# Two decoder layers over a long key and value cache, one core: queries by halves of w_q, finer loads between the layers, keys turned two quarters at a time

## The chip, the core and the metric

The kernel runs on one core of a Trainium2 chip. The metric is device time in microseconds (us) for one execution; smaller is better. The kernel before takes 649.24 us in the median of three runs (648.29 to 649.81). The engines are called TensorE (PE in the profile), VectorE (DVE), ScalarE (ACT), GpSimd (POOL) and SyncE (SP). SyncE issues all DMAs; sixteen DMA engines carry them out, each a sixteenth of every large load.

## The reference

Four sequences of one token each (x is 4 x 512) go through attention, a feed-forward block, and both once more with the same weights and the same cache:

```python
x = x + attention(layernorm(x), k_cache, v_cache, wq, wo)
x = x + ffn(layernorm(x), w_gate, w_up, w_down)
x = x + attention(layernorm(x), k_cache, v_cache, wq, wo)
x = x + ffn(layernorm(x), w_gate, w_up, w_down)

# attention: 32 query heads, 8 key/value heads, 8192 cached positions, head size 128
q = x @ wq                          # 4 x (32 x 128)
p = softmax(q k^T * 128 ** -0.5)    # a group of 4 query heads shares one key head
return (p @ v) @ wo

# ffn: inner size 1792
return (silu(x @ w_gate) * (x @ w_up)) @ w_down
```

All tensors are bfloat16. The keys and values of all sequences are 67 MB each and are needed in both layers; the little that on-chip memory can keep from one layer to the next is kept, the rest is read twice. Nearly all of the 273 MB that the kernel reads is keys and values.

## The kernel before

**Tiles and slots.** The work of a layer is 16 units; a unit u is one sequence and two key heads (`pair_gb`). Its keys K(L, u) and its values V(L, u) are one tile each of 128 partitions by 32 KB (4096 KB). On chip, `kvf` has four slots of that size and a fifth, number `QS`, which holds w_q until the second layer's queries are made and is a fifth slot of the ring from then on. Each slot is divided into eight blocks (`NB = 8`, "quarters" in the change's words), named `s<slot>.<block>`; a block is 512 KB. A small remainder behind the slots holds part of w_up. The feed-forward weights of layer 0 and 1 go into the slots `W_SLOT = (1, 3)`.

**Order of the loads.** `cmds` (L346 to L364) is a list, written out once, of all loads in order: tile, slot, first and last block. `pump` (L405) issues from its head as long as the blocks that the next load needs are free, and stops at the first that is not; so all loads keep this order on SyncE's queue. `freed(s, a, b)` marks blocks free and pumps; it is called in the program where the last reader of those blocks has been emitted, and the load then waits on semaphores for that reader. At the change of layers the list goes: the weights of layer 0's feed-forward, the second keys' tile of layer 1 into slot 1 (as 3, 1 and 4 blocks), the third into slot `QS` (as 4 and 2 blocks), the fourth into slot 0 (as 4 and 4), the third unit's predecessor's values into slot 1 (as 4 and 4), and then whole tiles in turn.

**What is kept between the layers.** The order of units in layer 1 begins with the last ones of layer 0 (`order`, L322). The keys of the last unit stay in slot 0, turned already, and become layer 1's first tile; two values' tiles stay too. Of one more keys' tile, K(0, NP - 3), the last two blocks are moved into PSUM by `hold(q, False)`, and brought back into slot `QS` by `hold(q, True)` after the queries of layer 1 are made. Bringing back overwrites w_q's place, so it waits for what was last recorded on the names "wq0" and "wq1" (`WQ`):

```python
if back:                                                              # L450
    T._wait("dve", T._need((), WQ))
    T.op("dve", lambda e: e.transpose(w, banks), reads=there, writes=here)   # L452
```

`_need` (L31) collects, for each name, its last writer and the readers since. A name's last writer is whatever operation or load listed it last in `writes`; `load` (L424) lists both names of `WQ` with the first load that goes into slot `QS`.

**A unit's keys.** `keys` (L598) takes a tile's eight blocks in turn. VectorE turns a block in place (`turn`, L488: 32 x 32 transposes of 4-byte words, 128 x 1024); TensorE then makes the scores of that block with four matmuls (`scores`, L512) into one PSUM bank. After the eighth block VectorE takes the maximum (L518), TensorE turns it (L523), VectorE reduces it (L526), TensorE spreads it (L554, later L549), VectorE forms the bias (L557), ScalarE the exponentials (L559), and VectorE turns those (L576). `values` then multiplies them with the values' tile (L643), VectorE gathers the parts (L689, L693). The scores of a block run behind its turning by a lag (`LAG`, and `AHEAD` for the second tile of layer 1, which lets all its eight blocks be turned first); `line` holds the small steps above and spaces them by estimated times. Every engine takes its instructions strictly in the emitted order.

**Queries.** `qproj` (L833) makes the queries of all heads: for each of 32 heads four matmuls over the four 128-row parts of w_q (L839), two of which lie in each half of the slot. In the middle stands `deviation` (L826), the layer norm's scale. In layer 0 it waits for both loads of w_q.

**Feed-forward.** `ffn` (L861) does gate, up (L876) and down (L907, in three groups of `WDS`) and frees blocks 0 to 2 after gate, block 3 after up, and blocks 4 to 7 after all of down. In layer 1 the down matmuls are those of L897.

Of the kernel before, what the change touches and what calls it, by code (L numbers as in the profile page):

```python
# [9 lines left out]
FP32 = mybir.dt.float32  # L10
# [93 lines left out]
def bass_interleave_layers__gqa_block_cached__swiglu_ffn__decode_kernel(  # L104
# [20 lines left out]
    KT = D // P  # L125
# [19 lines left out]
    with ExitStack() as es:  # L145
# [50 lines left out]
        def room(s, a, b):  # L196
            return [f"s{s}.{q}" for q in range(a // BW, (b - 1) // BW + 1)]
# [137 lines left out]

        ends = lambda it, s: [(it, s, 0, QH), (it, s, QH, NB - 1), (it, s, NB - 1, NB)]
        half = lambda it, s: [(it, s, q, q + NB // 2) for q in range(0, NB, NB // 2)]

        def placed(seq, ring, parts):
            out = []  # L340
            for i, it in enumerate(seq):
                s = ring[i % len(ring)]
                out += parts[i](it, s) if i in parts else [(it, s, 0, NB)]
            return out
# [10 lines left out]

        us = order[1]
        s = W_SLOT[0]
        cmds += [(K(1, us[1]), s, 0, 3), (K(1, us[1]), s, 3, 4), (K(1, us[1]), s, 4, NB)]
        cmds += [(K(1, us[2]), QS, 0, NB // 2), (K(1, us[2]), QS, NB // 2, NB - 2)]
        seq = loads(1, 3)  # L360
        ring = (0, 1, 3, QS, 2)
        cmds += placed(seq, ring, {0: half, 1: half, len(seq) - 1: ends})
        assert W_SLOT[1] == ring[len(seq) % len(ring)]
        cmds += [(("W", 1), W_SLOT[1], 0, NB), (("W+", 1), W_SLOT[1], NB, NB + 1)]  # L364

# [58 lines left out]
        def load(it, a, b, sm):  # L424
            kind, L, u = it
            s = slot_of[it]
            gp, bt = pair_gb(u)
            src = (A_k_cache if kind == "K" else A_v_cache)[bt, 2 * gp:2 * gp + 2, :, :].rearrange(
                "h (p t) d -> (h p) (t d)", t=TT)
            over = WQ if s == QS and not q_gone else []  # L430
            q_gone.update(over)
            T.dma("sp", kv[:, s, a * BW:b * BW], src[:, a * BW:b * BW], sm,
                  writes=[f"s{s}.{q}" for q in range(a, b)] + over)
# [46 lines left out]
                line.pop(0)[2]()  # L480


        def turn(L, u, q):


            s = slot_of[K(L, u)]
            w = kv[:, s, q * BW:(q + 1) * BW].bitcast(FP32)
            T.op("dve", lambda e: e.transpose(w, w), reads=[f"s{s}.{q}"], writes=[f"s{s}.{q}"])  # L488
            turned.add((L, u, q))

        placed_q = set()

# [105 lines left out]
        def keys(L, u, before, lag):  # L598
            def block(q):
                if q == 0:  # L600
                    place_q(L, u)
                scores(L, u, q)
                finished(K(L, u), q, q + 1)
                if q == NB - 1:
                    step = lambda gap, fn: [gap, u, lambda: fn(u)]
                    line.extend([step(0.0, max_p), step(1.2, max_t)])
                    after = [step(0.9, exps), step(1.3, lambda u: turn_p(L, u))]
                    if u == order[L][-1]:
                        after = [after[0], step(0.3, lambda u: turn_p(L, u)), [2.5, None, lambda: total(u)]]
                    (line if before is None else behind.setdefault(before, [])).extend(after)  # L610

            drain(lag)
            for q in range(NB):
                if (L, u, q) not in turned:
                    turn(L, u, q)
                blocks.append((0.9, lambda q=q: block(q)))
                drain(lag)

# [213 lines left out]

        def qproj(L, u):  # L833
            at, name = place("ln", 0, Hq * B)
            for h in range(Hq):
                if h == Hq // 2:
                    deviation(lsc_sb, "lsc")
                for kt in range(KT):
                    T.op("pe", lambda e: e.matmul(at[:, h * B:(h + 1) * B],  # L839
                                                  lhsT=wq_sb[:, kt, h * Dh:(h + 1) * Dh],  # L840
                                                  rhs=xn[:, kt * B:(kt + 1) * B],
                                                  start=(kt == 0), stop=(kt == KT - 1)),
                         reads=[f"wq{kt // 2}", "xn"], writes=[name], sig=(kt == KT - 1))
# [14 lines left out]
            place_q(L, u, "dve", ob, [oname])  # L858
            T.op("dve", lambda e: e.tensor_copy(qr, ob), reads=[oname], writes=["qr", "made"])

        def ffn(L):  # L861
# [3 lines left out]
            uT = bank(ub)[:, 0:FO * B]  # L865
            fb = lambda ap: ap.rearrange("p (f b) -> p f b", b=B)
            rb = rstd[:].unsqueeze(1).to_broadcast([P, FO, B])
            rooms = {"wg": room(s, 0, O_WU), "wu": room(s, O_WU, O_WD), "wd": room(s, O_WD, O_WD + FO * D)}
            names = {"wg": ["wg"], "wu": ["wu0", "wu1", "wu2"]}
            for at, wname, bk in ((wg_at, "wg", gb), (wu_at, "wu", ub)):  # L870
                for fo in range(FO):
# [19 lines left out]
            if L == 1:  # L891
                x_rows(1)
                for i, (a, b, _) in enumerate(WDS[1]):
                    for fo in range(a, b):
                        for j in range(NA):
                            o = s * SL + O_WD + fo * D + j * P
                            T.op("pe", lambda e: e.matmul(quarter(j), lhsT=hT[:, fo * B:(fo + 1) * B],  # L897
                                                          rhs=kvf[:, o:o + P], start=False, stop=(fo == FO - 1)),
                                 reads=["hT", f"wd{i}"] + rooms["wd"], writes=[f"part{j}"],
                                 sig=(fo == b - 1))  # L900
                freed(s, 4, NB)
                return
            for j, (a, b, _) in enumerate(WDS[0]):
                k = OBK[0] if j else SBK[1]
                for nt in range(KT):
                    for fo in range(a, b):
                        T.op("pe", lambda e: e.matmul(bank(k)[:, nt * B:(nt + 1) * B],  # L907
                                                      lhsT=wd_at(s, fo, nt),
                                                      rhs=hT[:, fo * B:(fo + 1) * B],
                                                      start=(j < 2 and nt == 0 and fo == a),  # L910
                                                      stop=(j in (0, NW - 1) and nt == KT - 1 and fo == b - 1)),
                             reads=["hT", f"wd{j}"] + rooms["wd"], writes=[f"pb{k}"], sig=(fo == b - 1))
                if not j:
                    add_to_x(bank(k)[:, 0:XB], f"pb{k}")
            freed(s, 4, NB)
            add_to_x(bank(k)[:, 0:XB], f"pb{k}")


# [10 lines left out]
        for L in range(2):  # L929
            us = order[L]  # L930
            turn_of.update((u, i % 2) for i, u in enumerate(us))
            totals.clear()
            mixed.clear()
            center()
            qproj(L, us[0])
            if L:
                for q in (NB - 2, NB - 1):
                    hold(q, True)
                freed(QS, 0, NB - 2)
            todo = [("K", 0)]  # L940
# [51 lines left out]
```

## Time and profile before

| what | value |
|---|---|
| median of three runs | 649.24 us (648.29 to 649.81) |
| the profiled execution | 648.29 us |
| its span, first to last instruction | 646.5 us |
| read from HBM | 272.9 MB, 422 GB/s over the span |
| DMA queue of SyncE | busy 99.0% of 16 engines' span |
| PE, DVE busy | 425.6 us (66%), 430.1 us (67%) |
| mean granted TensorE clock | 0.876 |
| L488, a block turned | 246 times, 1219 ns each |
| L512, a score matmul | 1024 times, 426 ns each |

The profile divides the span into 40 slices of 16.2 us; layer 0's attention ends at about 339 us, its feed-forward runs from there to 351 us, the queries of layer 1 from 352.6 to 357 us. In a group of instructions the first number is busy time, then the mean of one in ns; the idle time stands after the bar, with what ended most of it. In the chain of waits each line is a start, a length, and the engine, tile and line. For DMAs the number behind the size is the median time from the issue on SyncE to the landing on the last of the DMA engines, which includes the time that a load waits behind others.

### The profile page before, as it was taken

To read this page: it belongs to the slowest core of one execution; us is meant where nothing else is said; L and a number is where in the kernel's file an instruction comes from. 1 tells how busy PE (TensorE), PEld (TensorE's weight loads), DVE (VectorE), ACT (ScalarE), POOL (GpSimd) and SP (SyncE) were. 2 spreads that over 40 slices of the span, in tenths; PEclk is the share of its full clock that TensorE was granted. 3 is DMA by queue.
4 is the path that set the end of the run, shared out by engine and by line. 5 is a ranking of instruction groups with operands and counts; after the bars stand their busy time and mean duration, and the time that the engine had idled before them with its cause. 6 is when DMAs were issued, how large, how long until landed. Compare 5 with 4: busy or idle time off the path is not lost.

```text
span 646.5 us, 7503 instructions
## 1 busy us (share of the span) xinstructions
PE 425.6 (66%) x3128; PEld 173.1 (27%) x3128; DVE 430.1 (67%) x706; ACT 41.2 (6%) x117; POOL 11.1 (2%) x43
## 2 busy tenths in 40 slices
PE   2574466556766755767757987777665576657878
PEld 2221122212322212222226332222222222222225
DVE  1585467566776666777852878888766677766953
ACT  1000000000000000001010010000000000000110
POOL 0000000000000000000000000000000000000000
PEclk9996896789787999878985799999878997789977
DMA  9999999999999999999999999999999999999996
GB/s 363 445 423 416 442 429 430 426 435 433 426 430 435 430 425 436 435 422 436 434 407 409 396 435 434 434 429 423 442 427 426 433 438 424 431 440 423 430 417 268
DMA packets 14129, 273.37 MB, mean 423 GB/s; under 512 B 1416, under 2 KB 1424, under 8 KB 5264
## 3 DMA queue, kind: packets, MB, share of 16 engines
q1 hardware_dynamic: 14096, 272.91, 99.0%
q8 instruction: 24, 0.39, 0.2%
q14 instruction: 9, 0.07, 0.0%
HBM read 272.90 MB, written 0.00 MB: 422 GB/s over the span
## 4 chain that ended last, share of the span: by engine, by line
DMA 61%; DVE 26%; PE 9%; issue 3%; SPq 0%; ACT 0%; DVEq 0%
DMA kvf<-in_A_k_cache_dram 49%; DVE kvf L488 20%; DMA kvf<-in_A_v_cache_dram 10%; PE ps L512 3%; DVE pT L576 3%; PE ps L643 2%; DMA kvf<-in_B_w_down_dram 2%; DVE pb L693 2%; PE ps L839 1%; DVE pb L689 0%; PE ps L876 0%; DVE scr L703 0%; DVE kvf L452 0%; PE ps L759 0%; SPq L93 0%
## 5 line engine op out<-in xcount | busy, mean ns | idle before, releaser
L512 PE MATMUL ps<-kvf,zq 128*128 128x512 bf16 x1024 | 298.0, 426 | 181.1 <-DVE kvf L488 174.3
L488 DVE STREAM_TRANSPOSE kvf<-kvf 128x1024 f32<-128x1024 f32 x246 | 289.8, 1219 | 108.6 <-DMA kvf<-in_A_k_cache_dram 107.7
L512 PEld LDWEIGHTS ps<-kvf,zq 128*128 128x128 bf16 x1024 | 90.6, 105 | 350.9 <-DVE kvf L488 257.8
L643 PE MATMUL ps<-kvf,pT 128*32 128x512 bf16 x960 | 66.7, 400 | 1.4 <-DVE pT L576 0.8
L559 ACT ACTIVATE pb<-ps,tiny 128x512 bf16<-128x512 f32 x32 | 22.0, 688 | 531.8 <-DVE tiny L557 495.2
L576 DVE STREAM_TRANSPOSE pT<-pb 64x512 bf16<-64x512 bf16 x60 | 41.2, 687 | 3.1 <-ACT pb L559 2.0
L518 DVE TENSOR_REDUCE tiny<-ps 128x1 f32<-128x512 f32 x32 | 22.0, 687 | 31.6 <-PE ps L512 31.6
L693 DVE SCALAR_TENSOR_TENSOR pb<-ps,tiny,pb 128x128 f32<-128x128 f32 x104 | 36.5, 351 | 5.1 <-PE ps L643 1.3
L643 PEld LDWEIGHTS ps<-kvf,pT 128*32 128x32 bf16 x960 | 20.8, 98 | 31.9 <-issue 15.7
L698 PEld LDWEIGHTS ps<-sel,pb 128*128 128x128 f32 x64 | 15.4, 258 | 21.3 <-DVE pb L693 14.0
L502 POOL TENSOR_TENSOR zq<-scr,tiny 128x64 bf16<-128x64 bf16 x30 | 9.0, 300 | 564.8 <-PE ps L512 564.8
L526 DVE TENSOR_REDUCE mrm<-ps 1x8 f32<-1x128 f32 x32 | 8.8, 275 | 14.2 <-PE ps L523 14.2
L698 PE MATMUL ps<-sel,pb 128*128 128x8 f32 x64 | 12.7, 272 | 8.1 <-DVE pb L693 8.1
L549 PEld LDWEIGHTS ps<-mrm,tiny 128*128 128x128 f32 x60 | 12.0, 205 | 8.6 <-DVE scr L703 3.2
L759 PE MATMUL ps<-wo_sb,scr 128*4 128x512 bf16 x48 | 11.0, 379 | 1.5 <-DVE scr L728 1.5
L689 DVE TENSOR_SCALAR pb<-ps,tiny 128x128 f32<-128x128 f32 x32 | 10.1, 315 | 2.6 <-PE ps L643 2.6
L549 PE MATMUL ps<-mrm,tiny 128*128 128x16 f32 x60 | 9.3, 231 | 3.1 <-ACT mrm L561 3.1
L839 PE MATMUL ps<-xn,kvf 128*128 128x4 bf16 x256 | 7.6, 166 | 3.8 <-DMA kvf<-in_A_wq_dram 3.0
L561 ACT ACTIVATE mrm<-head,tiny 128x8 f32<-128x8 f32 x32 | 9.6, 301 | 1.0
L523 PE MATMUL ps<-identf,tiny 128*1 128x128 f32 x32 | 8.6, 270 | 0.2 <-DVE tiny L518 0.2
L839 PEld LDWEIGHTS ps<-xn,kvf 128*128 128x128 bf16 x256 | 7.6, 106 | 4.0 <-DMA kvf<-in_A_wq_dram 3.1
L876 PE MATMUL ps<-xn,kvf 128*128 128x4 bf16 x224 | 7.3, 169 | 1.8 <-DMA kvf<-in_B_w_up_dram 1.4
(83 smaller groups left out, 113.9 us busy)
## 6 DMA issues: line engine op xcount, KB each, us to landing
kvf<-in_A_k_cache_dram SPq DMA_DIRECT2D x28, 4096.0 KB, 30.8
kvf<-in_A_v_cache_dram SPq DMA_DIRECT2D x27, 4096.0 KB, 32.9
kvf<-in_A_v_cache_dram SPq DMA_DIRECT2D x4, 2048.0 KB, 20.0
kvf<-in_A_k_cache_dram SPq DMA_DIRECT2D x4, 2048.0 KB, 10.0
kvf<-in_A_wq_dram SPq DMA_DIRECT2D x2, 2048.0 KB, 9.8
wo_sb<-in_A_wo_dram SPq DMA_DIRECT2D x4, 1024.0 KB, 40.6
kvf<-in_B_w_gate_dram SPq DMA_DIRECT2D x2, 1792.0 KB, 24.5
kvf<-in_A_v_cache_dram SPq DMA_DIRECT2D x2, 1536.0 KB, 34.8
```

The lines of the kernel that those rows point to most:

```text
L488: T.op("dve", lambda e: e.transpose(w, w), reads=[f"s{s}.{q}"], writes=[f"s{s}.{q}"])
L512: T.op("pe", lambda e: e.matmul(bank(bk)[:, 0:SW], lhsT=zq[:, z0:z0 + P], rhs=w[:, :, c // 2, :, c % 2], start=(q == 0 and c == 0), stop=( ...
L518: T.op("dve", lambda e: e.tensor_reduce(mx[:], bank(bk)[:, 0:SW], AX.X, ALU.max), reads=[f"pb{bk}"], writes=["mx"])
L549: T.op("pe", lambda e: e.matmul(at, lhsT=ones, rhs=mrm[:, i * H2:(i + 2) * H2], start=True, stop=True), reads=[f"m8{i}", "rsm", "onesf"], ...
L559: T.op("act", lambda e: e.activation(pb[:], bank(bk)[:, 0:SW], ACTF.Exp, bias=nm, accum_out=rs), reads=[f"pb{bk}", "nm"], writes=PB + ["rs"])
L576: T.op("dve", lambda e: e.transpose(dst, pb[hp]), reads=["pb", "row"], writes=[name])
L643: T.op("pe", lambda e: e.matmul(bank(k)[j * QB:(j + 1) * QB, q0 * Dh:q1 * Dh], lhsT=p_t[:, t, h, :], rhs=v[:, q0:q1, t, :], start=((last o ...
L689: T.op("dve", lambda e: e.tensor_scalar(into, o, own[:, q:q + 1], None, op0=ALU.mult), reads=[f"pb{k}", "own"], writes=["row"] if last els ...
L693: T.op("dve", lambda e: e.scalar_tensor_tensor(into, o, own[:, q:q + 1], into, op0=ALU.mult, op1=ALU.add), reads=[f"pb{k}", "own", iname], ...
L698: T.op("pe", lambda e: e.matmul(at, lhsT=into, rhs=sel[:], start=True, stop=True), reads=[iname, "sel"], writes=[name])
L759: T.op("pe", lambda e: e.matmul(bank(OUTB)[0:B, 0:D], lhsT=oT[:, h, :], rhs=wo_sb[:, h, :], start=(gp == groups[L][0] and r == 0), stop=(g ...
L839: T.op("pe", lambda e: e.matmul(at[:, h * B:(h + 1) * B], lhsT=wq_sb[:, kt, h * Dh:(h + 1) * Dh], rhs=xn[:, kt * B:(kt + 1) * B], start=(k ...
```

## The change

- `qproj` runs over the two halves of w_q in its outer loop: the first two parts for all heads, `deviation`, then the last two parts for all heads. All 32 heads accumulate in one PSUM bank, which is opened by the very first matmul and closed by the last. In layer 1 the first half of slot `QS` is freed after the first half.
- `load` lists of `WQ` only the half that a load overwrites: the load of blocks 0 to 3 lists "wq0", that of blocks 4 and 5 lists "wq1".
- The second keys' tile of layer 1 is loaded as 3, 1, 2 and 2 blocks; the fourth as four times 2 (`twos`).
- In `ffn` each group of w_down has its own block names, and in layer 0 blocks 4 and 5 are freed after the first group, 6 and 7 after the last.
- `turn` takes a number of blocks. All tiles but the first and the last of each layer are turned two blocks at a time, as one instruction of 128 x 2048.

```diff
+        twos = lambda it, s: [(it, s, q, q + 2) for q in range(0, NB, 2)]
...
-        cmds += [(K(1, us[1]), s, 0, 3), (K(1, us[1]), s, 3, 4), (K(1, us[1]), s, 4, NB)]
+        cmds += [(K(1, us[1]), s, a, b) for a, b in ((0, 3), (3, 4), (4, 6), (6, NB))]
         cmds += [(K(1, us[2]), QS, 0, NB // 2), (K(1, us[2]), QS, NB // 2, NB - 2)]
...
-        cmds += placed(seq, ring, {0: half, 1: half, len(seq) - 1: ends})
+        cmds += placed(seq, ring, {0: twos, 1: half, len(seq) - 1: ends})
...
-            over = WQ if s == QS and not q_gone else []
+            over = [w for i, w in enumerate(WQ) if s == QS and a // (NB // 2) == i and w not in q_gone]
             q_gone.update(over)
             T.dma("sp", kv[:, s, a * BW:b * BW], src[:, a * BW:b * BW], sm,
                   writes=[f"s{s}.{q}" for q in range(a, b)] + over)
...
-        def turn(L, u, q):
+        def turn(L, u, q, n):
             s = slot_of[K(L, u)]
-            w = kv[:, s, q * BW:(q + 1) * BW].bitcast(FP32)
-            T.op("dve", lambda e: e.transpose(w, w), reads=[f"s{s}.{q}"], writes=[f"s{s}.{q}"])
-            turned.add((L, u, q))
+            w = kv[:, s, q * BW:(q + n) * BW].bitcast(FP32)
+            names = [f"s{s}.{i}" for i in range(q, q + n)]
+            T.op("dve", lambda e: e.transpose(w, w), reads=names, writes=names)
+            turned.update((L, u, i) for i in range(q, q + n))
...
-                    turn(L, u, q)
+                    two = 0 < order[L].index(u) < NP - 1 and q % 2 == 0 and (L, u, q + 1) not in turned
+                    turn(L, u, q, 1 + two)
...
-            for h in range(Hq):
-                if h == Hq // 2:
+            for c in range(2):
+                if c:
                     deviation(lsc_sb, "lsc")
-                for kt in range(KT):
-                    T.op("pe", lambda e: e.matmul(at[:, h * B:(h + 1) * B],
...
+                for h in range(Hq):
+                    for kt in (2 * c, 2 * c + 1):
+                        T.op("pe", lambda e: e.matmul(at[:, h * B:(h + 1) * B],
...
+                if L and not c:
+                    freed(QS, 0, NB // 2)
...
-            rooms = {"wg": room(s, 0, O_WU), "wu": room(s, O_WU, O_WD), "wd": room(s, O_WD, O_WD + FO * D)}
+            rooms = {"wg": room(s, 0, O_WU), "wu": room(s, O_WU, O_WD)}
+            for j, (a, b, _) in enumerate(WDS[L]):
+                rooms[f"wd{j}"] = room(s, O_WD + a * D, O_WD + b * D)
...
                 if not j:
+                    freed(s, 4, 6)
                     add_to_x(bank(k)[:, 0:XB], f"pb{k}")
-            freed(s, 4, NB)
+            freed(s, 6, NB)
...
-                freed(QS, 0, NB - 2)
+                freed(QS, NB // 2, NB - 2)
```

More of the change, by code (lines that the diff above doesn't have):

```diff
@@ L834, in qproj @@
             at, name = place("ln", 0, Hq * B)
-            for h in range(Hq):
-                if h == Hq // 2:
+            for c in range(2):
+                if c:
                     deviation(lsc_sb, "lsc")
-                for kt in range(KT):
-                    T.op("pe", lambda e: e.matmul(at[:, h * B:(h + 1) * B],
[L840 to L843, printed above, removed]
+                for h in range(Hq):
+                    for kt in (2 * c, 2 * c + 1):
+                        T.op("pe", lambda e: e.matmul(at[:, h * B:(h + 1) * B],
+                                                      lhsT=wq_sb[:, kt, h * Dh:(h + 1) * Dh],
+                                                      rhs=xn[:, kt * B:(kt + 1) * B],
+                                                      start=(kt == 0 and h == 0), stop=(kt == KT - 1 and h == Hq - 1)),
+                             reads=[f"wq{c}", "xn"], writes=[name], sig=(kt % 2 == 1 and h == Hq - 1))
+                if L and not c:
+                    freed(QS, 0, NB // 2)
             T.op("dve", lambda e: e.tensor_tensor(qT, at.rearrange("p (h b) -> p b h", b=B),
@@ L898, in ffn @@
                                                           rhs=kvf[:, o:o + P], start=False, stop=(fo == FO - 1)),
-                                 reads=["hT", f"wd{i}"] + rooms["wd"], writes=[f"part{j}"],
+                                 reads=["hT", f"wd{i}"] + rooms[f"wd{i}"], writes=[f"part{j}"],
                                  sig=(fo == b - 1))
@@ L911, in ffn @@
                                                       stop=(j in (0, NW - 1) and nt == KT - 1 and fo == b - 1)),
-                             reads=["hT", f"wd{j}"] + rooms["wd"], writes=[f"pb{k}"], sig=(fo == b - 1))
+                             reads=["hT", f"wd{j}"] + rooms[f"wd{j}"], writes=[f"pb{k}"], sig=(fo == b - 1))
                 if not j:
+                    freed(s, 4, 6)
                     add_to_x(bank(k)[:, 0:XB], f"pb{k}")
-            freed(s, 4, NB)
+            freed(s, 6, NB)
             add_to_x(bank(k)[:, 0:XB], f"pb{k}")
```

## The prediction

> **What bounds the kernel now.** I read the slices of the page first, then its list of DMA issues, then the chain of waits between 340 and 400 us, then single issues and windows of the same stretch. The slices and the issues come first:
>
> ```profile
> DMA  9999999999999999999999999999999999999996
> GB/s 363 445 423 416 442 429 430 426 435 433 426 430 435 430 425 436 435 422 436 434 407 409 396 435 434 434 429 423 442 427 426 433 438 424 431 440 423 430 417 268
> ...
> kvf<-in_A_k_cache_dram SPq DMA_DIRECT2D x28, 4096.0 KB, 30.8
> ```
>
> The reader sees DMA engines that never rest. A 4096 KB tile needs 9.7 us of transfer (the landings of neighbouring tiles in the trace lie 9.7 us apart), so a median of 30.8 us from issue to landing means that some 20 us of other loads lie ahead of it. In such a stretch nothing that VectorE or TensorE gains or loses by a few us reaches the end. Only around the change of layers (slices 21 to 23: 407, 409, 396) is the rate lower. There I read the chain:
>
> ```profile
> 358.06 2.29 DVE kvf L452 x2
> 360.35 9.01 DVE kvf L488 x8
> 369.36 0.59 DVE tiny L518
> 369.99 0.27 PE ps L523
> 370.26 0.87 PE ps L512 x4
> 371.13 0.31 PE ps L554 x2
> 371.44 4.46 PE ps L512 x20
> 375.90 0.98 PE ps L643 x16
> ```
>
> This is a compute chain with no DMA in it: hold() brings two kept quarters back (L452), VectorE turns the eight quarters of the second tile, then takes the maximum of the first tile (L518), and TensorE, which has L523 in its order behind the first two quarters' scores, goes on with the rest. SyncE's issues in this stretch hang on it:
>
> ```profile
> 345.06 22.62 SPq L93 DMA_DIRECT2D kvf<-in_A_k_cache_dram  x7
> 372.50 3.81 SPq L93 DMA_DIRECT2D kvf<-in_A_v_cache_dram  x2
> 378.16 0.33 SPq L93 DMA_DIRECT2D kvf<-in_A_k_cache_dram  x1
> ```
>
> The last view is of single issues, each asked for by its own window: the 512 KB and the 2048 KB half of the second keys' tile (issued 348.35 and 351.19), the first load into w_q's slot (356.71) and the first half of the values (372.50); the last number is issue to last landing.
>
> ```profile
> kvf<-in_A_k_cache_dram SPq DMA_DIRECT2D x1, 512.0 KB, 7.3
> ...
> kvf<-in_A_k_cache_dram SPq DMA_DIRECT2D x1, 2048.0 KB, 9.4
> ...
> kvf<-in_A_k_cache_dram SPq DMA_DIRECT2D x1, 2048.0 KB, 9.0
> ...
> kvf<-in_A_v_cache_dram SPq DMA_DIRECT2D x1, 2048.0 KB, 11.8
> ```
>
> They land at 355.7, 360.6, 365.7 and 384.3. Each transfer ends on the slowest of 16 DMA engines; the landing records show the fastest some 3 us ahead (381.3 against 384.3 for the values). The early engines run dry near 352, 358 and 366; the slowest hardly does (360.6 less 355.7 is 4.9, the plain time of 2048 KB).
>
> **The change part by part.** *Queries by halves.* The same 128 small matmuls (166 ns, 1.87 us for each 64), in another order. After the first 64 the first half of w_q's slot is free, so its load goes out at 352.64 + 1.87 = about 354.6 instead of 356.71. On SyncE it stands behind only loads that go out by 351.3. In the first layer the reordering is hidden: the first keys land at 24.2 us, 10 us after w_q.
>
> *Finer loads.* The last 2048 KB of the second keys' tile become two of 1024 KB, the first free after L907's first group (349.95 instead of 351.19); the fourth keys' tile becomes four loads instead of two, the first out at about 361.3 instead of 363.87. In the packet records a 16 KB packet takes 611 ns and an 8 KB one 309, so the 48 smaller packets of each engine cost it about 0.2 us, plus three more issues of 0.33 us on SyncE beside running transfers. The gain is what the early engines lose now. Windows of 5 us from 340 to 370 show 409, 419, 395, 368, 410, 397 GB/s; against 430 that is 2.1 us, of which about 0.9 is the small packets of the weights. So 1.2 us, at most 1.4, if nothing else ran dry.
>
> *Pairs.* The trace has no transpose of 2048 columns. One of 512 columns (L576) takes 687 ns, one of 1024 takes 1204, so 517 more per 512 columns: 2238, or about 2.2 us in a row of them. Its bounds are 1.20 (no growth) and 2.41 (two of 1204); I take 2.2, by the slope. Some 100 pairs then save 0.07 us each against 2 x 1.13, and hold the first quarter's scores back by 1.1 us. Both lie under the 20 us queue. In the chain above four pairs take 8.8 instead of 9.0.
>
> *The wait that the change adds.* hold() makes VectorE wait for the last writers of both w_q halves. So far these are the w_q loads, long landed. In the changed code the first half of w_q's slot is given to the next keys inside the query projection, before hold() is emitted, and that load is recorded as the new writer of "wq0". The built code bears it out: the first returning transpose now waits for the semaphore of that 2048 KB key load, which it does not read. When does that load land? On the slowest engine 355.7 + 4.9 (two 1024 KB) + 4.9 = 365.5; before, the transfer in the same place landed at 365.7. That engine is not short of work, so the earlier issue doesn't move it. VectorE sits from 358.0 to 365.5.
>
> Behind it in VectorE's order stand the two returns (2.3, to 367.8), four pairs (8.8, to 376.6), L518 (0.7, to 377.3). TensorE finishes the first tile's scores at 367.3 as before, does two quarters of the second, and stands at L523 until 377.3. Then L523 (0.3), a quarter, L554, a quarter: 380.1 at full clock (1.04 us a quarter) or 381.6 at half (1.7). The row of a window after a rest tells which:
>
> ```profile
> 95.00:100.00 5.00, 0.00 (x0) 0.00 (x0) 0.00 (x0) 0.00 (x0) 0.00 (x0) 0.65 0.99 426
> 100.00:105.00 5.00, 3.62 (x10) 1.56 (x10) 4.82 (x8) 0.00 (x0) 0.00 (x0) 0.50 1.00 433
> ```
>
> After 5 us without a matmul the next 5 ran at 0.50. TensorE rests some 5 us here, so I take 381.4. The Trainium skill, TensorE: Matmul & The Clock Gate, Part 1, says the same with a limit: half rate after one idle window of about 3.4 us, full again after a busy one, with a phase that varies from run to run. By it alone the quarter could be either value; this trace agrees with the half.
>
> SyncE then issues the values' first half at 381.4, not 372.5; queued behind it are the second half (after the last quarter, 386.2 instead of 375.98), the next keys (388.3 instead of 378.16) and all that follows. What lies ahead of it, the fourth keys' tile, is through by 374.1 on the fastest engine and 377.4 on the slowest. All 16 run dry, for 4 us and more. A load into dry engines: the one of 356.71 had its first landing mark after 7.4 us and its last after 9.0. I take 8.1: it lands at 389.5 instead of 384.3, **+5.2**. The bounds are 380.1 + 7.4 and 381.6 + 9.0, so +3.2 to +6.3. By the Trainium skill's DMA: Bandwidth & Descriptors, Anatomy of one DMA, which gives about 2.0 us plus bytes at 436 GB/s, it would be 6.8 and the landing 388.2, thus +3.9; both landing marks here are later.
>
> The second half goes out about 2.5 us before the first is through. A lead of 2.3 us, at 363.87, cost most engines nothing and four some 1.3: 0 to 1.3, I take **+0.3**. Later leads are over 3 us. The 3 us spread between engines closes in the dry spell, where before the slowest carried it on: 0 to -0.9, I take **-0.4**. The early issues' 1.2 us is worth nothing, since the engines that won it wait all the same.
>
> Sum: +5.1 us on the profiled run's 648.29 (span 646.5 and 1.79 around it) is 653.4. That run is 0.95 below the median of the three shown, 649.24; against the median it is **654.3**.
>
> **The rivals.** *Faster: the wait is hidden.* The early issues alone give -1.3, **647.9**. For it speak the dips in the rate; against it, the sum of what stands behind the wait. The values' half went out at 372.5, and the slowest engine ran to 378.9; less 2.5 for a start from dry, it could go out up to 3.9 us later at no cost. So this decides if the key load landed by about 361.4. The two loads ahead of it and its own end at 365.5 on the slowest engine.
>
> *Much slower: the lead stays gone.* The third tile's last pair comes one transpose later and TensorE stays late, so the values of the third tile (389.06 before, about 400.5 now) miss the end of the next keys' transfer at some 404 too, and each pair of tiles loses again: +2 to +3 more, **657**. For it, that this lead is only 3 us; against it, that compute needs 15 us a tile after this (the chain repeats at 390.5 and 405.5) where DMA needs 19.4, so it regains 4 us per tile.
>
> *No change.* The wait falls on work that the queue covers to within a us: **649**. It needs the same 3.9 us, only half passed.
>
> **How the numbers follow.** The forecast 0.80, much slower 0.12, faster 0.04, no change 0.04. The range 651.4 to 657.4 runs from the low bounds (+3.2 - 0.9, about 651.5) to the high ones (+6.3 + 1.3, 656.8) and takes in the slow rival. 0.2% (1.3 us) is about what a measurement of this kernel can tell from no change: faster 0.04, same 0.04, slower 0.92.
>
> **What would show it.** In the new profile: VectorE idle some 7 us ahead of the first returning transpose, released by a key load; that transpose at 365 to 366; L518 near 377; the values' first half issued at 380 to 382; a hole in DMA share and GB/s between 375 and 384; before 340 and after 400 the rates as now; pairs at 2.2 us. I am wrong if the return starts near 358, if the DMA rate has no hole, or if the issues of the second layer run with the old lead throughout.

## The result and the profile after

| | before | after |
|---|---|---|
| median | 648.6 us (647.47 to 649.81, 6 runs) | 654.85 us (654.5 to 655.41, 6 runs) |
| ratio, 95% interval | | 1.0096 [1.0083, 1.0109] |
| the profiled execution, its span | 648.29, 646.5 | 655.01, 653.1 |
| SyncE's DMA queue busy | 99.0% | 98.0% |
| mean granted TensorE clock | 0.876 | 0.835 |

The change makes the kernel 6.25 us slower by the medians, and 6.6 us by the spans of the two profiles. First the page of the kernel after: the slices, the turned keys among the groups, and the loads of whole keys' tiles among the issues.

```profile
DMA  9999999999999999999999959999999999999996
GB/s 376 426 424 420 439 434 427 424 439 424 437 427 433 428 431 432 425 437 427 423 413 412 411 239 444 425 438 423 435 428 428 438 421 442 424 432 432 423 421 269
...
L488 DVE STREAM_TRANSPOSE kvf<-kvf 128x2048 f32<-128x2048 f32 (+1 forms) x135 | 280.3, 2102 | 125.0 <-DMA kvf<-in_A_k_cache_dram 124.9
...
kvf<-in_A_k_cache_dram SPq DMA_DIRECT2D x28, 4096.0 KB, 31.1
```

There is one hole, in slice 24: 239 GB/s where 435 stood. Against 435 a slice of 16.3 us that moves 239 has lost 16.3 x (1 - 239/435) = 7.3 us of transfer. Slices 21 to 23 went from 407, 409, 396 to 413, 412, 411: a little better. Elsewhere the rates are about as before, and a whole tile still takes some 31 us from issue to landing. The chain of waits through the hole:

```profile
354.66 11.06 DMA kvf<-in_A_k_cache_dram
365.74 2.38 DVE kvf L453 x2
368.12 8.77 DVE kvf L488 x4
376.89 0.59 DVE tiny L518
377.52 0.37 PE ps L523
377.89 1.71 PE ps L512 x4
379.59 0.52 PE ps L554 x2
380.12 5.57 PE ps L512 x20
```

Before, the chain through this stretch, from the queries over the returns at 358.06 to the values, had no DMA in it. Now a DMA of 11 us stands ahead of the returns: the load of the third keys' tile into the first half of w_q's slot, issued at 354.66 and landed at 365.7. VectorE's waits between 340 and 420 us (total, times, longest) have it as their largest, once:

```profile
DVE kvf L453 <- DMA kvf<-in_A_k_cache_dram: 7.6, 1, 7.6
```

What SyncE could issue behind that, by the timeline (start, length, number of issues):

```profile
382.01 4.08 SPq L93 DMA_DIRECT2D kvf<-in_A_v_cache_dram  x2
387.94 0.33 SPq L93 DMA_DIRECT2D kvf<-in_A_k_cache_dram  x1
```

The values go out at 382.01 instead of 372.50, the next keys at 387.94 instead of 378.16. The windows of 5 us show what the DMA engines did meanwhile (behind the length stand the busy times of TensorE, its weight loads, VectorE, ScalarE and GpSimd; the last three columns are the granted clock of TensorE, the DMA share and GB/s):

```profile
370.00:375.00 5.00, 1.91 (x8) 0.69 (x8) 5.00 (x4) 0.00 (x0) 0.00 (x0) 1.00 0.98 406
375.00:380.00 5.00, 2.48 (x7) 1.02 (x7) 2.74 (x3) 0.00 (x0) 0.00 (x0) 0.55 0.22 90
380.00:385.00 5.00, 5.00 (x19) 2.02 (x20) 1.58 (x4) 1.08 (x3) 0.00 (x0) 0.76 0.42 134
385.00:390.00 5.00, 3.26 (x39) 1.05 (x37) 3.73 (x5) 0.00 (x0) 0.30 (x1) 1.00 0.99 426
```

By the packet records the engines run out of work one after another between 375 and 377.6 us, no data moves from there until 383.0, about 1 us behind the issue at 382.01, and from 384 the rate is full again.

**Where the time went, engine by engine.** The landing records give, for each load, the time at which each of the 16 DMA engines reported its share. From each such mark I take away the time that an engine needs for its sixteenth of all packets up to there (by the packet records, a packet of each size at its usual time); what is left is how far the engine is behind an engine that never rests. Below is this lateness, averaged over the 16 engines and for the slowest, at three loads. With another average of the packet times (they are recorded in whole ns) a single figure moves by up to 0.4 us.

| us behind | before, mean | before, slowest | after, mean | after, slowest |
|---|---|---|---|---|
| the 512 KB keys' load, issued at 348.4 | 3.62 | 5.45 | 3.56 | 5.50 |
| the values' first half | 5.05 | 7.01 | 11.36 | 11.66 |
| the last load of the kernel | 5.39 | 7.70 | 11.62 | 13.92 |

On the mean engine the stretch between the first two rows cost 1.43 us before and costs 7.80 now, 6.37 more. By the last load it is 6.23, about the loss that was measured (6.25 by the medians, 6.6 by the spans). On the slowest engine the values' half is only 4.65 later by this count, and the rest (to 6.22) comes after it. This difference is the subject of one of the points below.

### The profile page after: what moved, and what is told of

Read it like the earlier page. It is cut to its first block, busy times and chain, and to the rows that moved or that the text cites. A ratio compares the mean times of both kernels' runs of the same rounds, so it can differ in the third digit from the quotient of the medians.

```text
span 653.1 us, 7416 instructions
## 1 busy us (share of the span) xinstructions
PE 419.6 (64%) x3126; PEld 181.4 (28%) x3128; DVE 421.9 (65%) x595; ACT 41.2 (6%) x117; POOL 11.2 (2%) x43
## 4 chain that ended last, share of the span: by engine, by line
DMA 62%; DVE 21%; PE 12%; issue 3%; SPq 0%; ACT 0%; ACTq 0%; DVEq 0%
DMA kvf<-in_A_k_cache_dram 51%; DVE kvf L488 17%; PE ps L512 8%; DMA kvf<-in_B_w_gate_dram 5%; DMA kvf<-in_A_v_cache_dram 4%; DMA kvf<-in_B_w_down_dram 2%; PE ps L644 2%; DVE pb L694 1%; DVE pT L576 1%; PE ps L882 0%; DVE pb L690 0%; DVE ps L456 0%; DVE kvf L453 0%; PE ps L523 0%; PE ps L903 0%
## 5 line engine op out<-in xcount | busy, mean ns | idle before, releaser
L488 DVE STREAM_TRANSPOSE kvf<-kvf 128x2048 f32<-128x2048 f32 (+1 forms) x135 | 280.3, 2102 | 125.0 <-DMA kvf<-in_A_k_cache_dram 124.9
L512 PEld LDWEIGHTS ps<-kvf,zq 128*128 128x128 bf16 x1024 | 100.0, 109 | 350.5 <-DVE kvf L488 231.7
L518 DVE TENSOR_REDUCE tiny<-ps 128x1 f32<-128x512 f32 x32 | 22.0, 686 | 21.7 <-PE ps L512 21.7
L699 PEld LDWEIGHTS ps<-sel,pb 128*128 128x128 f32 x64 | 16.9, 272 | 16.5 <-DVE pb L694 8.0
L523 PE MATMUL ps<-identf,tiny 128*1 128x128 f32 x32 | 8.7, 273 | 6.4 <-DVE tiny L518 6.4
```

Source lines behind the costliest of these rows:

```text
L488: T.op("dve", lambda e: e.transpose(w, w), reads=names, writes=names)
L512: T.op("pe", lambda e: e.matmul(bank(bk)[:, 0:SW], lhsT=zq[:, z0:z0 + P], rhs=w[:, :, c // 2, :, c % 2], start=(q == 0 and c == 0), stop=( ...
L518: T.op("dve", lambda e: e.tensor_reduce(mx[:], bank(bk)[:, 0:SW], AX.X, ALU.max), reads=[f"pb{bk}"], writes=["mx"])
L699: T.op("pe", lambda e: e.matmul(at, lhsT=into, rhs=sel[:], start=True, stop=True), reads=[iname, "sel"], writes=[name])
```

## The experiments

The theory under test (A): the wait that hold() now has for a key load it does not read makes the whole loss. The main rival (B): the finer loads, the pairs or the new order cost time of themselves. All kernels below compute the whole reference. In the table the ratio is to the kernel before on the same chip; "V" is the issue of the first half of the values of layer 1's third unit, the load into slot 1 behind the fourth keys' tile, and the last three columns are the mean lateness, as above, at the 512 KB load, at the values' first half and at the last load, from one profile each.

| run | median, us | ratio, 95% | V issued | lateness |
|---|---|---|---|---|
| before | 648.6 | | 372.50 | 3.62, 5.05, 5.39 |
| after | 654.85 | 1.0096 [1.0083, 1.0109] | 382.01 | 3.56, 11.36, 11.62 |
| e1_wq1_only | 647.24 | 0.9980 [0.9972, 0.9989] | 372.48 | 3.57, 4.01, 4.28 |
| e2_wait_alone | 655.54 | 1.0105 [1.0087, 1.0124] | 382.44 | 3.82, 12.16, 12.86 |
| e3_half_dose | 652.31 | 1.0057 [1.0041, 1.0073] | 379.43 | 3.54, 8.66, 9.11 |
| e4_single_turns | 655.25 | 1.0103 [1.0087, 1.0119] | 382.02 | 3.60, 11.49, 12.24 |
| e5_wait_in_slack | 649.22 | 1.0015 [1.0006, 1.0024] | 376.32 | 3.73, 5.76, 6.05 |
| e6_wq1_single | 647.92 | 0.9991 [0.9983, 1.0000] | 372.26 | 3.59, 3.55, 3.87 |
| e7_wq1_coarse | 647.37 | 0.9991 [0.9982, 1.0000] | 372.03 | 3.63, 4.14, 4.44 |
| e8_values_quarters | 647.21 | 0.9982 [0.9973, 0.9991] | 369.53 | 3.56, 3.59, 3.79 |
| e9_pairs_alone | 648.38 | 0.9993 [0.9984, 1.0003] | 372.22 | 3.59, 4.66, 4.97 |
| e10_halves_alone | 648.21 | 0.9994 [0.9984, 1.0003] | 372.67 | 3.95, 4.95, 5.34 |
| e11_all_three | 647.13 | 0.9980 [0.9971, 0.9989] | 372.77 | 3.72, 3.91, 4.17 |

### The wait taken away: e1_wq1_only

The kernel after, but the returns wait for the readers and the load of the second half of w_q's place only. This stays free of races because blocks 6 and 7, where the quarters return, lie in the second half alone.

```diff
-                T._wait("dve", T._need((), WQ))
+                T._wait("dve", T._need((), WQ[1:]))
```

> The changed kernel, with the returns in hold() waiting for the name wq1 alone (the blocks they overwrite lie in that half), so no longer for the key load that took over wq0. Theory A (that wait makes the whole loss): the first return starts near 358 us as in the kernel before, the values' first half goes out near 373 us instead of 382.0, there is no hole in the DMA rate, and the time falls by 6 to 8 us to about 647.4, ratio to before 0.996 to 1.000. Rival B (smaller loads, pairs or the other order of the queries cost the time): 652 us or more, ratio 1.004 or more.

Measured: 647.24 us, 0.9980 [0.9972, 0.9989]. Its timeline:

```profile
358.19 2.37 DVE L453 STREAM_TRANSPOSE kvf<-ps 128x1024 f32<-128x1024 f32 x2
...
372.48 3.81 SPq L93 DMA_DIRECT2D kvf<-in_A_v_cache_dram  x2
```

The returns start at 358.19 without a wait, the values go out within 0.02 us of before, and the hole is gone (442 GB/s between 375 and 380). One wait carries the whole loss: 7.6 us of time lie between this kernel and the kernel after. What remains of the change is worth 0.2%.

### The wait alone, put into the kernel before: e2_wait_alone

The kernel before, with none of the three parts of the change; only the first load into slot QS is emitted ahead of the returns, so that it becomes the last writer of w_q's names.

```diff
             if L:
+                freed(QS, 0, NB - 2)
                 for q in (NB - 2, NB - 1):
                     hold(q, True)
-                freed(QS, 0, NB - 2)
```

> The kernel before, with the two blocks of code swapped at the change of layers: the slot of w_q is freed, so its first key load recorded, ahead of hold(). Neither finer loads, nor pairs, nor queries by halves. Theory A: the first return waits for that load (landing near 365.7), L518 comes near 377, the values' first half is issued near 382, and the time is 5 to 7 us above before, ratio 1.008 to 1.011, like the whole change. Rival B: within 1 us of before, ratio 0.9985 to 1.0015.

Measured: 655.54 us, 1.0105 [1.0087, 1.0124].

```profile
365.92 2.38 DVE L452 STREAM_TRANSPOSE kvf<-ps 128x1024 f32<-128x1024 f32 x2 [7.72 <-DMA kvf<-in_A_k_cache_dram]
...
382.44 4.83 SPq L93 DMA_DIRECT2D kvf<-in_A_v_cache_dram  x2
```

The same wait (7.72), nearly the same late issue (382.44), and a loss whose interval overlaps that of the whole change. With e1 this shows both directions: without the wait no loss, with nothing but the wait the loss. Rival B falls here, and with e4.

### Single turns in the kernel after: e4_single_turns

```diff
-                    turn(L, u, q, 1 + two)
+                    turn(L, u, q, 1)
```

> The changed kernel, but keys turned one quarter at a time as before. Theory A: the wait stays and eight turns of 1.13 us stand where four of 2.2 us stood, so L518 comes 0.2 us later; the time is within 0.7 us of the changed kernel, ratio to before 1.0085 to 1.0110. Rival B in its form that pairs cost (they hold back the first quarter's scores by 1.1 us in each tile): faster than the changed kernel by over 2 us, ratio under 1.006.

Measured: 655.25 us, 1.0103 [1.0087, 1.0119], an interval that overlaps that of the kernel after. The eight turns behind the wait, in its timeline:

```profile
367.81 9.08 DVE L488 STREAM_TRANSPOSE kvf<-kvf 128x1024 f32<-128x1024 f32 x8
```

9.08 us for eight singles against 8.85 for four pairs in the kernel after (2.21 a pair). The pairs neither make the loss nor hide a part of it that could be measured.

### Half the wait: e3_half_dose

The kernel after, with the third keys' tile loaded two blocks at a time, so that the load with the name "wq0" is 1024 KB and lands earlier.

```diff
-        cmds += [(K(1, us[2]), QS, 0, NB // 2), (K(1, us[2]), QS, NB // 2, NB - 2)]
+        cmds += [(K(1, us[2]), QS, q, q + 2) for q in range(0, NB - 2, 2)]
```

> The changed kernel, with the first load into w_q's slot cut into two of 1024 KB; the returns wait for the first of them alone. Theory A: it lands 2.4 us earlier (near 363.3), and as all engines are dry in any case, the issue of the values (near 379.6) and the end move by the same 2.4 us: 652.4 us, ratio 1.0055 to 1.0065. Rival B: no change or slightly slower for the smaller packets, ratio 1.0095 or more. Rival C (the loss is set by a fixed cost of a dry start, not by the length of the wait): ratio 1.009 to 1.010.

Measured: 652.31 us, 1.0057 [1.0041, 1.0073].

```profile
363.15 2.38 DVE L453 STREAM_TRANSPOSE kvf<-ps 128x1024 f32<-128x1024 f32 x2 [5.25 <-DMA kvf<-in_A_k_cache_dram]
...
379.43 4.81 SPq L93 DMA_DIRECT2D kvf<-in_A_v_cache_dram  x2
```

The wait is 2.4 us shorter, the values go out 2.58 us earlier, the kernel is 2.54 us faster: one for one in this range.

### A wait inside the slack: e5_wait_in_slack

The prediction's rival "the wait is hidden" said that the values could go out up to 3.9 us later at no cost. Here e1 waits for the last load of the second keys' tile, which lands at 360.5, ahead of the 361.4 that the prediction named as deciding.

```diff
-                T._wait("dve", T._need((), WQ[1:]))
+                T._wait("dve", T._need([f"s{W_SLOT[0]}.{NB - 1}"], WQ[1:]))
```

> The kernel of e1_wq1_only (returns freed of the key load), with another wait in its place: the returns wait for the last quarters of the second keys' tile, which land near 360.8 us. VectorE is held up by about 2.5 us instead of 7.6. Theory A with its threshold of 3.9 us (the values may go out that much later before the slowest DMA engine runs dry): the values are issued near 375 us, the early engines may lose up to 1 us, the end nothing, within 0.6 us of e1_wq1_only, ratio to before 0.997 to 0.9995. Rival (loss in proportion to the wait, 6.3 us for 7.6): 2.1 us over e1_wq1_only, ratio 1.0010 to 1.0025.

Measured: 649.22 us, 1.0015 [1.0006, 1.0024]: 1.98 us above e1's 647.24, so the wait was not free. In its timeline the wait is 2.63 us, but the values go out 3.84 us later than in e1:

```profile
360.57 2.38 DVE L453 STREAM_TRANSPOSE kvf<-ps 128x1024 f32<-128x1024 f32 x2 [2.63 <-DMA kvf<-in_A_k_cache_dram]
...
376.32 3.92 SPq L93 DMA_DIRECT2D kvf<-in_A_v_cache_dram  x2
```

The returns begin 2.38 us later than in e1 (360.57 against 358.19; e5 had reached this point 0.3 us earlier), and L518 begins 2.38 us later too (371.64 against 369.26). The rest of the 3.84, 1.46 us, arises between L518 and the issue (4.68 us, 3.22 in e1), where TensorE works, and goes with its clock. TensorE stood idle for 2.65 us ahead of L523 (0.35 in e1), and windows of 1 us show the granted clock (third column from the end) at half afterwards, while the quarters whose end frees the values' slot were being computed: a quarter of 1.03 us in e1 takes 1.45 here.

```profile
371.00:372.00 1.00, 0.00 (x0) 0.00 (x0) 1.00 (x2) 0.00 (x0) 0.00 (x0) 1.00 0.98 401
372.00:373.00 1.00, 0.65 (x4) 0.40 (x5) 0.57 (x2) 0.00 (x0) 0.00 (x0) 0.96 1.03 418
373.00:374.00 1.00, 1.00 (x4) 0.17 (x1) 0.00 (x0) 0.00 (x0) 0.00 (x0) 0.50 1.07 451
...
375.00:376.00 1.00, 1.00 (x3) 0.29 (x2) 0.46 (x1) 0.80 (x3) 0.00 (x0) 0.50 0.55 229
376.00:377.00 1.00, 1.00 (x5) 0.43 (x4) 0.95 (x2) 0.00 (x0) 0.00 (x0) 0.83 0.43 180
```

So 3.84 us of delay cost 1.98. Of the slack of 3.9 us that I had worked out, only some 1.9 was there. By the time alone the other case of the expectation, a loss in proportion to the wait (2.1 us), would do as well. The lateness speaks for a slack that was smaller. The last keys' load ahead of the values was done at 376.6 on the mean engine and at 377.8 on the slowest; the prediction had taken 2.5 us for a start from dry and the slowest engine. A start takes 2.0 us here (6.8 from issue to the first landing mark, less 4.9 of transfer), so the values would have had to go out at 374.6 to cost the mean engine nothing. They were 1.7 us late by that, and the mean lateness rose by 1.84 from the load ahead to the values (3.92 to 5.76), while that of the slowest rose by 0.8 only (5.14 to 5.95). Kernel e8 below points the same way: its values go out 3 us earlier than e1's and it gains nothing, so not every us of that issue counts.

### The three parts without the harmful wait: e6, e7, e8

Each is e1 with one more edit. e6 turns the keys one block at a time (queries by halves and finer loads are left):

```diff
-                    turn(L, u, q, 1 + two)
+                    turn(L, u, q, 1)
```

> The kernel of e1_wq1_only, with keys turned one quarter at a time. If pairs are hidden under the queue, as predicted: within 0.5 us of e1_wq1_only, ratio to before 0.997 to 0.999. If pairs carry the gain of e1_wq1_only: ratio 0.9995 to 1.001. If they cost: ratio under 0.997.

e7 has the loads as they were before (queries by halves and pairs are left):

```diff
-        cmds += [(K(1, us[1]), s, a, b) for a, b in ((0, 3), (3, 4), (4, 6), (6, NB))]
+        cmds += [(K(1, us[1]), s, a, b) for a, b in ((0, 3), (3, 4), (4, NB))]
...
-        cmds += placed(seq, ring, {0: twos, 1: half, len(seq) - 1: ends})
+        cmds += placed(seq, ring, {0: half, 1: half, len(seq) - 1: ends})
```

> The kernel of e1_wq1_only, with the loads as large as before (second keys' tile 3, 1, 4 blocks, fourth 4, 4). If the finer loads carry the gain, since they spare the early DMA engines their dry spells: most of the 1.2 us goes, ratio to before 0.999 to 1.001, and the rate from 350 to 370 us dips again below 410 GB/s. If the earlier first load of the queries' halves carries it: ratio 0.9975 to 0.999.

e8 goes further than the change and loads the first values in four parts too:

```diff
-        cmds += placed(seq, ring, {0: twos, 1: half, len(seq) - 1: ends})
+        cmds += placed(seq, ring, {0: twos, 1: twos, len(seq) - 1: ends})
```

> The kernel of e1_wq1_only, with the first values' tile of the second layer loaded as four of 1024 KB too, so that its first part goes out after two quarters of the second tile (near 370 us instead of 372.5). If the early engines are still short there: 0.3 to 0.7 us less than e1_wq1_only, ratio 0.9965 to 0.998. If the lead there is enough already: the same as e1_wq1_only within 0.5 us.

Measured, side by side: e6 0.9991 [0.9983, 1.0000], e7 0.9991 [0.9982, 1.0000], e8 0.9982 [0.9973, 0.9991]. e8's values go out 3 us earlier than e1's (369.53), for no gain over e1 that could be measured: in e1 the lateness does not rise across the values (4.03 on the last keys' load, 4.01 on the values), so nothing was left to win there. e6 and e7 both end between before and e1, within about 0.1% of either.

### Single parts of the change: e9, e10, and e1 once more

e9 is the kernel before with the new turn() and its pairs, and nothing else:

```diff
-                    turn(L, u, q)
+                    two = 0 < order[L].index(u) < NP - 1 and q % 2 == 0 and (L, u, q + 1) not in turned
+                    turn(L, u, q, 1 + two)
```

> The kernel before, with keys turned two quarters at a time and nothing else of the change. As predicted (the pairs lie under the queue of loads): within 0.5 us of before, ratio 0.9992 to 1.0008. If the longer hold of a pair's first quarter reached the end: over 1.001. If fewer VectorE instructions pay, as the 0.5 us between e6_wq1_single and e8_values_quarters may suggest: 0.9985 to 0.9992.

e10 is e7 with single turns, so that only the queries by halves and the early load into w_q's first half are left:

```diff
-                    turn(L, u, q, 1 + two)
+                    turn(L, u, q, 1)
```

> The kernel before, with the queries by halves and the early first load into w_q's slot, the returns waiting for wq1 alone; single turns, loads as large as before. If that early load alone spares the engines one of their three dry spells: 0.3 to 0.6 us less than before, ratio 0.9990 to 0.9996. If the dry spells of early engines never reach the end: 0.9997 to 1.0005.

e11 is e1 again, on the chip of e9 and e10:

> The kernel of e1_wq1_only again, beside the two parts alone on one chip. All parts together without the harmful wait: ratio 0.997 to 0.999 as there, 0.5 us or more below each part alone, if the parts add up; like the better of the two, if one carries it all.

Measured: pairs alone 0.9993 [0.9984, 1.0003], halves alone 0.9994 [0.9984, 1.0003], all three 0.9980 [0.9971, 0.9989]. Neither part alone can be told from no change; all three together can, and repeat e1's ratio. The lateness lost between the 512 KB load and the values points the same way (1.43 before; 1.07 pairs; 1.00 halves; 0.51 halves and pairs in e7; about none in e6; 0.2 and 0.4 in the two profiles with all three), but it is one profile each, and such a number moves by some tenths between profiles and with the packet times taken. It also doesn't put e6 and e1 in the order of their times. How the 0.2% divides among the parts stays open. The group of turned keys on e9's page:

```profile
L487 DVE STREAM_TRANSPOSE kvf<-kvf 128x2048 f32<-128x2048 f32 (+1 forms) x135 | 280.3, 2102 | 125.0 <-DMA kvf<-in_A_k_cache_dram 124.8
```

111 pairs and 24 single turns stand in place of 246 singles. VectorE is busy 421.8 us in all instead of 430.1, so a pair saves 8.3 / 111 = 0.07 us, as the prediction had it, and the end moves by nothing that can be measured.

One thing the pairs do move is TensorE's mean granted clock. In every run of a kernel with pairs (after, e1, e3, e5, e7, e8, e9, e11) it lies between 0.80 and 0.85, in every run of one with single turns (before, e2, e4, e6, e10) between 0.86 and 0.88. So the fall from 0.876 to 0.835 in the table of results goes with the pairs and not with the hole: e4, which has the hole and single turns, shows 0.862 to 0.874. In e9 it costs nothing that can be measured; why pairs lower it was not tested.

The best kernel of the study is the change with its wait corrected, e1 (0.9980 twice, on two chips), with e8 beside it (0.9982). It beats both the kernel before and the kernel after.

## Why the prediction was right, and where it was not

The forecast was 654.3 us, the result 654.85; slower, by the mechanism named. That the total came so close is in part luck, as the sum below shows. Step by step:

- **The false wait.** Predicted: VectorE idle from 358.0 to 365.5, for a key load that it does not read. Measured: 7.6 us idle, to 365.74. That this wait is the cause was shown in both directions (e1, e2).
- **The early issue doesn't move that landing.** The load went out at 354.66 (predicted 354.6) and landed at 365.7, as the transfer in its place did before. Right: the slowest engine was not short of work.
- **What stands behind the wait.** Returns 2.38 (2.3 predicted), four pairs 8.8 (8.8), L518 at 376.81 (376.6), V at 382.01 (381.4). TensorE's first quarter took 1.71 us, so half rate was the right choice; the window of 375 to 380 has the clock at 0.55. The issues behind it came at 385.76 and 387.94 (386.2 and 388.3).
- **A load into dry engines.** Predicted 8.1 us from issue to last landing, measured 7.3, with the first landing mark at 6.7. Here I had weighed a row of the trace, 7.4 to 9.0, against the Trainium skill's DMA: Bandwidth & Descriptors, Anatomy of one DMA, whose formula gave 6.8. The measurement lies between and nearer to the page; the page fits its formula to loads that GpSimd issues, and these are issued by SyncE, so the agreement may be chance. The row was of a load issued at 356.71, and the transfer ahead of it had its first landing mark at 357.87 only, so the row held some waiting too. By the later issue and the shorter landing the shift of that load came out at +5.0, predicted +5.2.
- **The second half's short lead.** Predicted +0.3, measured 0: it landed 4.9 us behind the first, the plain transfer time.
- **The spread between engines: the step that failed.** I took -0.4, arguing that the slowest engine, which had carried its lag through the kernel, starts level with the others after the dry spell. It did: the 16 marks of the values' first half lie within 0.6 us, against 3.0 before. But the lag did not stay closed. At the load that lands next after 404.7 us one of the 16 marks lies 1.6 us further behind, after 431.2 a second one, and by the last load the slowest is 2.3 us behind the mean again, as it was before the change (7.70 against 5.39; 13.92 against 11.62). In all thirteen profiles the slowest ends 1.6 to 2.7 us behind the mean, whatever happened in the middle. Before, new lags of single engines fell for some 200 us on engines that were not the slowest: the slowest one's lateness does not rise from the values to about 590 us. Once all engines are level, the first such lag makes a new slowest engine. So the advantage is lost again by the end, and the term is about +1.6 by the profiles in place of -0.4 (6.6 of span less 5.0 of landing), +1.25 by the medians.
- **The sum.** Predicted +5.1, measured +6.25 by medians. The forecast came out 0.55 from the result since its starting point, the median of three runs, was 0.64 above the median of six. Two misses, a sum 1.15 too small and a starting point 0.64 too high, thus lay in opposite directions; that half of the first was made up by the second is luck.
- **"The early issues are worth nothing."** Not contradicted in the kernel after, where all engines run dry anyway: e2, with the wait and no early issue, is within 0.7 us of it, and the intervals overlap. Worth 1.2 us, I had said, if nothing else ran dry; e1 gained 1.2 and e11 1.4 by the medians. But these have the pairs too. e6, which has the early issues without the pairs, gained 0.45 us (interval 0 to 1.1), so the agreement does not show that the early issues alone are worth 1.2.
- **The rivals.** "Much slower" fell: after the hole the mean lateness stays at 11.32 to 11.40 over the next loads, so no later pair of tiles lost again. "Faster" was not what this kernel did, but its price, a gain of 1.3 us (647.9 of 649.24), is about what e1 and e11 measured with the wait gone. Its deciding point, a landing by about 361.4, was wrong: in e5 the load landed at 360.6 and the wait still cost 2 us.

What failed in the spread and in the deciding point is one thing. Both were worked out on the slowest engine. On the mean engine, the difference in lateness between a kernel and the kernel before, at the values' first half, comes within 0.8 us of the change in span: +6.3 (span +6.6) after, +3.6 (+3.9) in e3, +0.7 (+0.5) in e5, -1.0 (-1.2) in e1, +7.1 (+7.9) in e2. The slowest engine gives +4.65, +1.85, -1.06, -1.52 and +5.5 for the same five. Over all twelve kernels compared with the one before, the mean engine comes within 0.9 us of the change in span, the furthest being e6 (-1.5, span -0.6). This is shown by the landing records.

What sets single engines back later goes with another kind of packet. The profile's list of queues has 24 packets of 16 KB that carry instructions,

```profile
q8 instruction: 24, 0.39, 0.2%
```

each of about 1.07 us, and two of them lie at 404.7 and 431.2 us, ahead of the two new lags named above. This is more than a coincidence of two. I compared each whole 4096 KB load with the load ahead of it, in all thirteen profiles and outside the change of layers. In 256 places some engine falls back by over 0.5 us against the others; in 239 of them a packet with instructions (these 24, or one of 8 KB on a further queue) started between the middle marks of the two loads. Of the 450 places without such a fall, 36 have one. So nearly all of the lags come with these packets. No run moved or removed one, so that the packets cause the lags is argued and not tested.

## What to carry to other kernels

When a change lets a transfer start earlier, look at whoever waits "for the last writer" of the place it overwrites: a wait that used to be for something long done becomes a wait for the new transfer, and costs the whole queue behind it, here 7.6 us of VectorE for blocks it never reads. In this kernel a gap in the transfers was worth what the average of the DMA engines lost and not what the last one lost, because a lead or a lag of single engines did not last to the end. Slack, too, counted here from the point where the mean engine runs dry, less the start of a transfer, and a delay of VectorE reached SyncE enlarged where TensorE lost its clock in between (2.4 us became 3.8 in e5).

## What the runs showed that I had not expected

- A rest of TensorE of 2.65 us (e5) was followed by half clock from 373 to about 376.3, some 3.4 us, with TensorE busy all that time; in e1 rests of 0.55 and 0.35 us left it at 1.00. The Trainium skill, TensorE: Matmul & The Clock Gate, Part 1, gives one idle window of about 3.4 us as the condition; the length of the half-rate stretch agrees, but here a rest shorter than that was enough.
- From issue to the first landing mark in engines that had run dry, 2048 KB took 6.7 us in the kernel after and 6.8 in e5, of which 4.9 is transfer: the start and the report of the landing cost about 1.9 us. In the kernel after, 1.0 of it lies between the issue and the first packet.
- The spread between the 16 engines is not a property that a kernel carries along: closed to 0.35 us in e5 and 0.6 us in the kernel after, it was back at 3.0 and 3.5 us at the last load, and nearly every new lag came with a packet that carries instructions, as counted above.
